# One-sided level scaling, token-layout keys for the state, and a re-sorted plan in a gated linear attention with a low-rank mixer

## The chip, the cores and the metric

The kernel runs on one core of one Trainium2 chip. The metric is the device time of one execution in microseconds; the median of three runs counts. The profile is of one further execution of the same program.

## The reference

Two blocks follow each other, all in float32. The first is a gated linear attention with a complex diagonal gate; B = 4 sequences, H = 8 heads, S = 768 tokens, D = 48 per head.

```python
mag = np.sqrt(a_re * a_re + a_im * a_im)
scale = np.minimum(mag, 0.999) / (mag + 1e-06)
a_re_n, a_im_n = (a_re * scale, a_im * scale)
for t in range(S):
    new_re = ar * S_re - ai * S_im
    new_im = ar * S_im + ai * S_re
    S_re, S_im = (new_re + kv, new_im)          # kv: outer product of k[t] and v[t]
    y[:, :, t] = np.einsum('bhd,bhde->bhe', q[:, :, t], S_re)
```

Its output, with heads side by side, is x with shape (4, 768, 384). The second block mixes tokens by a low-rank product (rank 32) and channels by two layers (384 to 1536 to 384):

```python
h = x.transpose(0, 2, 1) @ U @ V
u = x + h.transpose(0, 2, 1)
out = u + np.maximum(u @ w_ch1, 0.0) @ w_ch2
```

q, k, v and the gates are read with heads outermost. The two weight matrices arrive as 64-bit floats and are converted on the chip (`single`, from `stage` to `w`).

## The kernel before

**Chunks.** Each sequence is cut into chunks of 128 tokens: 24 chunks, 6 to a sequence. Chunks go in groups of two (`GROUPS`); `gates(g)` computes for a group the logarithm of the gate's size (`GL`) and its angle. `within` sums the logarithms from the middle of each block of eight tokens (matrix `mid`, tile `es ps`) and takes the exponentials in both signs (`es`, to scale q and k). `of_blocks` sums them over blocks of many sizes (matrix `total`, 64 columns; tile `tot`), takes the exponential (`E`) and a DMA brings it into the transposed layout as `T`. `angles` sums the angles (`ph`, `F`), and `waves_of` gives sine and cosine (`cs`).

**Prep.** `prep(i)` multiplies q and k by `es` (`weigh`), then by `cs` into `QKC` in token layout (128 tokens by 8 heads by 2 x 64), and TensorE transposes it (`tr`), ScalarE copying into `QK` (112 feature rows by tokens). Queries and keys share one `QKC` buffer.

**Chain.** `chain(i)` computes the causal products of a chunk by levels. After the products within the smallest blocks (`inner`), the queries and keys in `QK` are scaled by `T` so that blocks of double size fit; `times` scales a step of blocks, `grow` a whole level on both sides. There are five such multiplications on VectorE of 112 x 1024 elements for every chunk. The products go through masks into `DG`, by DMA into `AT`, and `corners` adds larger off-diagonal parts. When all scaling is done, the keys in `QK` refer to the end of each half chunk; TensorE transposes them back (`ks ps`), ScalarE copies them to `ks`, and `state` forms `dk` from them and the values `VP`. VectorE carries the running state: `GM` and `G` are the state times `T` plus `dk` (`onward`). `y` comes from `AT` with `VP` and from the queries with `G` and `GM`, and four ScalarE copies write `xo`.

**Mixer.** After each sequence, `mixer(m)` runs for its three pairs of chunks (12 pairs in all): `mixed` (low rank), `uTp`, then `up` and `down`. For the pairs m >= `FEWER` = 6, `up_fewer` replaces `up` by a scheme of 15 block products instead of 18 (tile `few`), with sums on VectorE into the `gate` area and `combine` for the weights. From the second pair on `down_two` does the same for the second layer.

**Order.** No engine's order is written by hand. `Plan` collects every operation with an engine, a cost, reads and writes, and a rank; `order` then runs a list scheduler over these costs and emits one fixed sequence for each engine. Ranks come from the `URGENCY` tables, one number for every stage and chunk. When TensorE has nothing ready before the first mixing, the plan emits a filler product (`spare`). Tiles with a `buffer` count or in a `ring` are handed on only when all their users are done. Semaphores do the waiting on the chip. From group `PAIRED` = 5 on, the levels of two chunks are issued together. Input and `T` transfers go by SyncE's queue, `out` mostly by GpSimd's.

A sequence's first chunk has no state before it, its last one makes none.

Of the kernel before, what the change touches and what calls it, by code (L numbers as in the profile page):

```python
# [26 lines left out]
    "w1": {0: 598.69, 1: 700.38, 2: 561.36, 3: -1085.13, 4: 936.46, 5: 518.46, 6: 1990.31},  # L27
    "w2": {0: 567.2, 2: 731.23, 4: 231.69, 6: 364.31, 8: -127.45, 10: 294.53, 12: 130.99},
    "gates": {0: 523.28, 1: -1082.8, 2: -1138.64, 4: -681.35, 6: 2038.0, 8: 706.57, 10: -2625.84, 12: -1988.48,
        14: 652.13, 16: 729.97, 18: -1261.2, 20: -1293.27, 22: -582.28},  # L30
    "angles": {0: -713.76, 1: 451.99, 2: -1094.23, 4: -1138.42, 6: -877.65, 8: -663.76, 10: 249.87, 12: 258.4,
        14: 730.71, 16: 600.46, 18: 890.52, 20: -1410.11, 22: -1050.09},
    "prep": {0: -1111.25, 1: -1273.83, 2: -1144.23, 3: -1283.97, 4: -1610.93, 5: -400.53, 6: -1090.46, 7: 47.1,
        8: -2361.51, 9: -1335.04, 10: -992.16, 11: -1290.23, 12: 355.91, 13: 718.13, 14: 425.49, 15: -1586.91,
        16: 164.12, 17: -2624.09, 18: -1995.12, 19: 1003.92, 20: 460.11, 21: 683.17, 22: 246.16, 23: 304.03},
    "levels": {0: -1274.23, 1: -77.35, 2: -1122.97, 3: 446.96, 4: -1027.24, 5: 563.68, 6: 533.1, 7: 540.33,
        8: 312.67, 9: -1060.71, 10: -1147.76, 11: 477.09, 12: 434.96, 13: 685.1, 14: 223.22, 15: -902.35,
        16: -1157.33, 17: 559.77, 18: -440.31, 19: 206.74, 20: -992.62, 21: -1506.01, 22: -990.49, 23: -1159.28},
    "rest": {0: 327.21, 1: -703.81, 2: 145.04, 3: 405.93, 4: -948.71, 5: -1277.74, 6: 399.6, 7: 573.79, 8: -1411.6,
        9: -1156.53, 10: -1047.5, 11: 209.25, 12: -915.97, 13: -1258.32, 14: -2795.59, 15: -1131.95, 16: -1080.72,  # L40
        17: -806.17, 18: 376.14, 19: -1093.98, 20: -1201.47, 21: 393.57, 22: -1199.57, 23: 107.96},
# [147 lines left out]
def kernel(  # L189
# [37 lines left out]
    FEWER = B * (S // CH) // 2 - 6  # L227
# [15 lines left out]
    SIZES = (4, 8, 16, 32, 64, 128)  # L243
    NTOT = CH // 2
# [107 lines left out]
    mid = singles.tile([128, CH], FP, name="mid")  # L352
    total = singles.tile([128, NTOT], FP, name="total")
# [32 lines left out]
    GL = [singles.tile([128, GC * DM + 64 - D], FP, name="GL")]  # L386
    nc.gpsimd.memset(GL[0], 0.0)

    tail = singles.tile([128, CH], FP, name="tail")
    nc.gpsimd.tensor_copy(out=tail, in_=ident[:, 127:128].to_broadcast([128, CH]))  # L390
    AT, DG, VP = [], [], []
    QKC = singles.tile([128, H, 2, DP], FP, name="QKC")
    nc.gpsimd.memset(QKC, 0.0)
    GATE = singles.tile([128, 6, GC * DM], FP, name="gate")
    AREA = {nm: GATE[:, n] for n, nm in enumerate(("x", "y", "n", "z", "ar", "ai"))}
# [14 lines left out]
    def constants():  # L410
# [8 lines left out]

        def totals():  # L420

            for n in SIZES:
                m, ends = CH // n, prefix.rearrange("p (b t) -> p b t", t=n)[:, :, n - 1]
                to = total[:, n // 4::n // 2]
                if n == 4:
                    to, frm = (a.rearrange("p (b x) -> p b x", x=4) for a in (to, ends))
                    for x in range(1, 4):
                        nc.gpsimd.tensor_tensor(out=to[:, :, (2, 1, 0, 3)[x]], in0=frm[:, :, x], in1=frm[:, :, x - 1],
                                                op=OP.subtract)
                    nc.gpsimd.tensor_copy(out=to[:, 0:1, 2], in_=frm[:, 0:1, 0])  # L430
                    nc.gpsimd.tensor_tensor(out=to[:, 1:, 2], in0=frm[:, 1:, 0], in1=frm[:, :-1, 3], op=OP.subtract)
                    continue
                nc.gpsimd.tensor_copy(out=to[:, 0:1], in_=ends[:, 0:1])
                if m > 1:
                    nc.gpsimd.tensor_tensor(out=to[:, 1:m], in0=ends[:, 1:m], in1=ends[:, 0:m - 1], op=OP.subtract)
# [28 lines left out]
    def single(p, rank, to, o, pieces):  # L464
# [23 lines left out]
        ACT(c_act(n), rank, lambda: act(o, hi().bitcast(FP), AF.Copy, scale=2.0 ** -112), [raw], [to])  # L488
        ACT(c_act(n), rank, lambda: act(word(x()), lo(), AF.Copy, scale=2.0 ** -29), [raw], [cx])
# [35 lines left out]
    def gates(g):  # L525


        x, y, l, n, z, ar, ai = names = [(nm, g) for nm in ("x", "y", "l", "n", "z", "ar", "ai")]
        first = GROUPS[g][0]

# [14 lines left out]
        def magnitudes_of(lo, hi):  # L545
            t, R1, W = t_of(lo, hi), ("gates", lo), (hi - lo) * DM
            ca, cd = c_act(W), c_dve(W)
            X, Y, L, N = (b + (lo,) for b in (x, y, l, n))
            AR, AI = ([b + (i,) for i in range(lo, hi)] for b in (ar, ai))
            ACT(ca, R1, lambda: act(t(x), t(ar), AF.Square), AR, [X])  # L550
            ACT(ca, R1, lambda: act(t(y), t(ai), AF.Square), AI, [Y])
# [13 lines left out]
            table(ca, R1, lambda: act(t(x), t(x), AF.Ln), [], [X])  # L565
            table(ca, R1, lambda: act(t(x), t(x), AF.Exp, scale=-1.0), [], [X])
            DVE(cd, R1, lambda: mul(t(x), t(x), t(ai)), AI, [X])
            ACT(ca, R1, lambda: act(t(n), t(ar), AF.Sign, bias=tiny), AR, [N])
            for i in range(lo, hi):
                within(i, R1, L)  # L570

# [80 lines left out]
        def waves():  # L652
            buffer(("cs", g), "cs", 2, [128, GC, H, 2, D])
            for part in PARTS[g]:
                waves_of(*part)
# [645 lines left out]
```

## Time and profile before

| | |
|---|---|
| median of three runs | 695.42 us (694.3 to 696.11) |
| the profiled execution | 695.63 us, span 693.8 us |
| TensorE busy | 668.7 us (96%), of it `spare` 53.3 us |
| VectorE busy | 521.5 us (75%), of it the levels' scaling (`QK`) 145.3 us |
| ScalarE busy | 432.1 us (62%), of it the copies to `ks` 23.8 us |
| GpSimd busy | 40.0 us (6%) |
| granted TensorE clock | 1.0 of full speed |

PE is TensorE, DVE VectorE, ACT ScalarE, POOL GpSimd, SP SyncE; PEld is TensorE's weight load, which overlaps its products. A stage line gives the stretch, its length, then busy time (and instruction count) of each engine, the clock, the share of the DMA engines and GB/s. A group line gives line number, engine, operation, tiles (out<-in), shapes and count, then busy time in total and the mean nanoseconds of one, and last the idle time before them with what ended it. Busy time of overlapping instructions is counted once, so busy divided by count can be below the mean of one.

### The profile page before, as it was taken

What the parts mean: (1) busy time and instruction counts of PE and PEld (TensorE: products, weight loads), DVE (VectorE), ACT (ScalarE), POOL (GpSimd) and SP (SyncE); (2) the same over time, 40 slices, a digit from 0 to 9 for tenths busy, and PEclk for the clock granted to TensorE, in tenths of its full rate; (3) what the DMA queues carried; (4) which work ended last, traced back from release to release, by engine and by line L of the source; (5) the groups of instructions that cost most, each with busy time, mean ns of one, the idle gap of its engine ahead of it and who ended that gap; (6) DMA issues with size and microseconds to landing.
All of it is one profiled execution on the core that took longest, in us unless ns stands there. A gap on an engine that the chain in (4) does not pass through costs nothing.

```text
span 693.8 us, 26918 instructions
## 1 busy us (share of the span) xinstructions
PE 668.7 (96%) x12098; PEld 590.5 (85%) x12098; DVE 521.5 (75%) x838; ACT 432.1 (62%) x802; POOL 40.0 (6%) x79
## 2 busy tenths in 40 slices
PE   7899887999999999999999999999999999999998
PEld 7788777786788887978988898889999989899998
DVE  4699998656989978946979588788797876465734
ACT  7999977679968887945968578634425315031230
POOL 5000000000101000010001001000000000000000
PEclk9999999999999999999999999999999999999999
DMA  8746435554514333251433222202111010000000
GB/s 203 187 94 161 90 76 119 131 163 113 114 35 95 80 73 83 47 110 26 78 85 67 49 65 57 60 20 58 26 42 24 14 33 10 23 2 24 7 18 24
DMA packets 163330, 48.32 MB, mean 70 GB/s; under 512 B 153808, under 2 KB 160016, under 8 KB 163216
## 3 DMA queue, kind: packets, MB, share of 16 engines
q1 hardware_dynamic: 161008, 42.26, 27.6%
q0 software_dynamic: 2208, 4.35, 1.8%
q8 instruction: 95, 1.56, 0.9%
q14 instruction: 19, 0.16, 0.1%
HBM read 33.59 MB, written 4.72 MB: 55 GB/s over the span
## 4 chain that ended last, share of the span: by engine, by line
PE 70%; ACT 19%; DVE 6%; issue 3%; DMA 1%; SPq 0%; DVEq 0%; ACTq 0%
PE down L1121 18%; PE few L990 12%; PE up L932 11%; ACT gate L327 7%; PE inner L732 4%; PE tr L698 4%; PE dk L818 3%; PE y L857 2%; ACT QK L701 2%; PE ks ps L803 2%; PE ph L643 2%; PE es ps L576 2%; ACT L324 2%; ACT GL L327 2%; PE y L849 2%
## 5 line engine op out<-in xcount | busy, mean ns | idle before, releaser
L330 DVE TENSOR_TENSOR QK<-QK,T 112x1024 f32<-112x1024 f32 x120 | 145.3, 1217 | 7.7 <-PE inner L732 4.2
L932 PE MATMUL up<-uT,w 128*128 128x256 f32 x432 | 99.2, 381 | 0.2 <-ACT h L327 0.2
L932 PEld LDWEIGHTS up<-uT,w 128*128 128x128 f32 x432 | 80.4, 190 | 12.7 <-ACT h L327 0.6
L1121 PE MATMUL down<-w,h 128*128 128x192 f32 x396 | 72.8, 329 | 1.1 <-issue 1.1
L327 ACT ACTIVATE gate<-gate 128x768 f32<-128x768 f32 (+1 forms) x91 | 70.3, 792 | 2.7 <-DMA gate<-in_a_re_dram 1.6
L701 ACT COPY QK<-tr 112x512 f32<-112x512 f32 x96 | 52.3, 587 | 31.0 <-PE tr L698 30.7
L998 ACT COPY h<-few 128x512 f32<-128x512 f32 x36 | 20.6, 585 | 81.9 <-PE few L990 77.1
L1121 PEld LDWEIGHTS down<-w,h 128*128 128x128 f32 x396 | 63.9, 190 | 3.6 <-issue 2.5
L333 DVE TENSOR_TENSOR h<-few,h 128x512 f32<-128x512 f32 x54 | 37.1, 690 | 34.7 <-PE few L990 33.4
L732 PEld LDWEIGHTS inner<-QK 112*32 112x32 f32 x4608 | 45.7, 109 | 14.1 <-issue 11.3
L732 PE MATMUL inner<-QK 112*32 112x16 f32 (+1 forms) x4608 | 51.2, 190 | 4.3 <-issue 3.0
L698 PE MATMUL tr<-ident,QKC 128*112 128x128 f32 x384 | 52.8, 276 | 2.3 <-DVE QKC L330 1.3
L1245 PE MATMUL spare<-ident 128*128 128x128 f32 x388 | 53.3, 285 | 1.4 <-POOL ident masks.py:199 1.4
L330 DVE TENSOR_TENSOR QKC<-qk,cs 128x768 f32<-128x768 f32 x48 | 45.7, 952 | 11.0 <-PE tr L698 9.0
L1245 PEld LDWEIGHTS spare<-ident 128*128 128x128 f32 x388 | 48.4, 197 | 4.9 <-POOL ident masks.py:199 1.4
L698 PEld LDWEIGHTS tr<-ident,QKC 128*112 128x112 f32 x384 | 41.9, 133 | 9.1 <-ACT QK L701 3.1
L333 DVE TENSOR_TENSOR xo<-down,xo 128x192 f32<-128x192 f32 (+1 forms) x79 | 29.5, 384 | 23.7 <-PE down L1121 23.4
L990 PE MATMUL few<-gate,w 128*128 128x128 f32 x336 | 43.5, 277 | 0.0
L866 ACT COPY xo<-y 64x192 f32<-64x192 f32 x96 | 29.9, 312 | 20.7 <-PE y L857 19.7
L990 PEld LDWEIGHTS few<-gate,w 128*128 128x128 f32 x336 | 40.0, 192 | 0.4
L327 ACT ACTIVATE h<-up 128x512 f32<-128x512 f32 x36 | 21.5, 596 | 29.7 <-PE up L932 29.6
L738 DVE COPY_PREDICATED DG<-mask,inner 128x128 f32<-128x128 int32 (+1 forms) x72 | 24.2, 341 | 17.3 <-PE inner L732 17.0
(130 smaller groups left out, 1241.7 us busy)
## 6 DMA issues: line engine op xcount, KB each, us to landing
stage<-in_moe_w_ch_dram SPq DMA_DIRECT2D x12, 768.0 KB, 5.6
gate<-in_a_re_dram SPq DMA_DIRECT2D x24, 192.0 KB, 3.6
gate<-in_a_im_dram SPq DMA_DIRECT2D x24, 192.0 KB, 3.5
qk<-in_q_dram SPq DMA_DIRECT2D x24, 192.0 KB, 2.7
qk<-in_k_dram SPq DMA_DIRECT2D x24, 192.0 KB, 4.0
VP<-in_v_dram SPq DMA_DIRECT2D x24, 192.0 KB, 3.2
T<-E SPq DMA_DIRECT2D x48, 96.0 KB, 2.5
AT<-DG SPq DMA_DIRECT2D x96, 32.0 KB, 2.1
```

Source lines behind the costliest of these rows:

```text
L327: return nc.scalar.activation(out=o, in_=i, func=f, **kw)
L330: nc.vector.tensor_tensor(out=o, in0=a, in1=b, op=OP.mult)
L333: nc.vector.tensor_tensor(out=o, in0=a, in1=b, op=OP.add)
L698: nc.tensor.transpose(out=get(*ps)[0:DQ, j], in_=get(*qkc)[:, hh * HH + j].rearrange("p u d -> p (u d)")[:, 0:DQ], identity=ident)
L701: ACT(c_act(HH * CH) - 0.05, R1, lambda u=u, hh=hh, ps=ps: nc.scalar.copy(out=get(*QK)[:, u, hh * HH:(hh + 1) * HH], in_=get(*ps)[0:DQ]), ...
L732: nc.tensor.matmul(out=get(*ps)[js, h], lhsT=k_of(h)[:, js], rhs=part(q_of(h)[:, js], "p"), start=True, stop=True, tile_position=(0, j * BLK))
L738: nc.vector.copy_predicated(out=to, mask=part(mask[:, n], "p").unsqueeze(1).to_broadcast(list(to.shape)), data=a if hf < 8 else a.rearrang ...
L866: ACT(c_act(HH * D), RR, lambda r=r, u=u: nc.scalar.copy(out=get(*xi).rearrange("p (a u d) -> p a u d", u=2, d=D)[r * HC:(r + 1) * HC, :, ...
L932: nc.tensor.matmul(out=get(*ps)[:, e], lhsT=w1[:, f, (ff + e) * 128:(ff + e + 1) * 128], rhs=get(*uT)[:, f], start=(f == 0), stop=(f == KD ...
L990: nc.tensor.matmul(out=get(*ps)[:, q], lhsT=w()[:, q * 128:(q + 1) * 128], rhs=v[0](), start=(n == 0 and q == 0), stop=True, skip_group_ch ...
L1121: nc.tensor.matmul(out=get(*to)[:, part], lhsT=x(j), rhs=y[:, j], start=(first and j == 0), stop=(j == KH - 1), skip_group_check=not first)
L1245: nc.tensor.matmul(out=spare[0], lhsT=ident, rhs=ident, start=True, stop=True)
```

## The change

It has these parts:

1. **Levels scale one side.** The `total` matrix has 28 columns instead of 64, for distances from the middle of one block to the middle of another. At each level either the queries or the keys are scaled, not both. A chunk has six multiplications of 512, 512, 512, 256, 512 and 1024 elements (512 for the first chunk of a sequence) instead of five of 1024.
2. **The state's keys are scaled in token layout.** A new matrix `fore` sums the logarithms from the middle of the block of eight to the end of the half chunk (product `ef ps`, one for each chunk, exponential `ef` on ScalarE). `onto_end` multiplies the keys in `QKC` in place, after they were transposed, and `state` takes them from there. The transposes `ks ps`, their copies and the tile `ks` are gone. `QKC` has two buffers, one for queries and one for keys. The state no longer waits for the levels.
3. **The first group's gates on VectorE** (`SPREAD`): the absolute value, the clamp of the logarithm, the sign and the last affine step, two instructions each, go from ScalarE to VectorE. The two conversion copies of the first three weights (`EARLY`) go there too.
4. **The seventh pair** (m = 6) computes `up` with 18 products (`FEWER` = 7).
5. Sine and cosine are made by chunk, with three buffers; `z` shares the area of `y`, and the area that `z` had holds part of `ef`; `tail` is a broadcast view of `ident`; `GL` has no padding; some costs of the plan differ by 0.05 to 0.1.
6. **All `URGENCY` numbers differ**, so the order on each engine differs throughout.

```diff
-    FEWER = B * (S // CH) // 2 - 6
+    FEWER = B * (S // CH) // 2 - 5
...
-    SIZES = (4, 8, 16, 32, 64, 128)
-    NTOT = CH // 2
+    EARLY, SPREAD = 3, (0,)
+
+    TA, TC, TQ, TK, TF, TH, NTOT = 0, 8, 12, 16, 18, 26, 28
...
-    QKC = singles.tile([128, H, 2, DP], FP, name="QKC")
-    nc.gpsimd.memset(QKC, 0.0)
+    QKC = []
+    for n in range(2):
+        QKC.append(singles.tile([128, H, 2, DP], FP, name="QKC%d" % n))
+        nc.gpsimd.memset(QKC[n], 0.0)
...
+        def ahead():
+
+            for r in range(0, CH, HC):
+                n = HC // 8
+                nc.gpsimd.tensor_tensor(
+                    out=fore[:, r:r + HC].rearrange("p (b t) -> p b t", t=8), in0=prefix[:, r + HC - 1:r + HC].unsqueeze(1).to_broadcast([128, n, 8]),
+                    in1=e[:, r // 8:r // 8 + n, 3:4].to_broadcast([128, n, 8]), op=OP.subtract)
+        POOL(0.7, ("load", 2), ahead, reads=[("prefix", 0)], writes=[("fore", 0)])
...
+            if p < EARLY:
+                DVE(one, rank, lambda o_=o_, i_=i_, scale=scale: nc.vector.tensor_scalar(
+                    out=o_(), in0=i_(), scalar1=scale, scalar2=None, op0=OP.mult), [raw], [at])
+            else:
+                ACT(c_act(n) + 0.1, rank, lambda o_=o_, i_=i_, scale=scale: act(o_(), i_(), AF.Copy, scale=scale), [raw], [at])
...
+            if on_dve:
+                DVE(c_one(W), R1, lambda: nc.vector.tensor_scalar(out=t(n).bitcast(U32), in0=t(ar).bitcast(U32), scalar1=0x7FFFFFFF, scalar2=None,
+                                                                  op0=OP.bitwise_and), AR, [N])
+            else:
+                ACT(ca, R1, lambda: act(t(n), t(ar), AF.Abs), AR, [N])
...
+            pf, ef = ("ef ps", i), ("ef", i)
+            psum(pf, "T", [128, DM], [128, 512])
+            summed(fore, ("fore", 0), pf, ef)
+            table(c_act(DM), R1, lambda: act(get(*ef), get(*pf), AF.Exp, scale=-1.0), [pf], [ef])
...
+        def onto_end():
+            a = get("qkc", 2 * i + 1)[:, :, :, 0:D]
+            mul(a, a, heads(get("ef", i)).unsqueeze(2).to_broadcast([128, H, 2, D]))
+        DVE(c_dve(2 * DM), ("rest", i), onto_end, [("ef", i)], [("qkc", 2 * i + 1)])
...
-        times(RL, 4, 16, 8, H * CH - 8, 0)
+        times(RL, 0, 8, TA, (16, 8, 1), (1, 8, 0))
         yield from inner(1, 8)
-        times(RL, 4, 16, 0, H * CH + 8, 2)
-        grow(RL, 8)
+        times(RL, 1, 0, TA, (16, 8, 1), (1, 8, 0))
+        times(RL, 0, 16, TC, (32, 4, 1), (1, 16, 0))
         yield from inner(0, 16)
...
-        grow(RR, 16)
+        times(RR, 1, 0, TK, (HC, 2, 1), (1, 16, 0))
+        times(RR, 0, 32, TQ, (HC, 2, 2), (16, 2, 1), (1, 16, 0))
...
-        grow(RR, 32)
+        lo = 0 if c else HC
+        times(RR, 0, lo, TF + lo // 16, (16, (CH - lo) // 16, 1), (1, 16, 0))
...
-        ks, dk = ("ks", i), [("dk", (i, r)) for r in range(2)]
-        buffer(ks, "ks", 1, [128, H, DQ])
+        ks, dk = ("qkc", 2 * i + 1), [("dk", (i, r)) for r in range(2)]
         buffer(mid_G, "GM", 1, [DQ, H, D])
-        rows_k = HC if last else CH
-        for hh in range(2):
-            ps = ("ks ps", (i, hh))
-            psum(ps, "A", [128, HH, DQ], [128, HH, CH])
-
-            def turn(hh=hh, ps=ps):
-                for j in range(HH):
-                    nc.tensor.transpose(out=get(*ps)[0:rows_k, j], in_=k_of(hh * HH + j)[:, 0:rows_k], identity=ident[0:DQ, 0:DQ])
-            PE(0.4, RR, turn, [QK], [ps], takes=[ks], steps=HH)
-            ACT(0.54, RR, lambda hh=hh, ps=ps: nc.scalar.copy(out=get(*ks)[0:rows_k, hh * HH:(hh + 1) * HH], in_=get(*ps)[0:rows_k]),
-                [ps], [ks + (hh,)])
...
-                        nc.tensor.matmul(out=get(*dk[r])[x:end, h], lhsT=get(*ks)[at, h, x:end], rhs=get(*VPi)[at, h],
+                        nc.tensor.matmul(out=get(*dk[r])[x:end, h], lhsT=get(*ks)[at, h, x // DP, 0:end - x], rhs=get(*VPi)[at, h],
```

In the listing of the changed program, all `ef` products for chunks 0 to 7 stand before the first `up`, and all 168 `spare` too; VectorE's instruction for the keys of a chunk stands behind `onto_end` of the chunk before.

## The prediction

> **What bounds the kernel now.** I read the page's busy shares and slices first, then the busy time by stage, the same stages for the `spare` products alone, the chain that ended last, and last the groups by form, for the price of single instructions. The page:
>
> ```profile
> PE 668.7 (96%) x12098; PEld 590.5 (85%) x12098; DVE 521.5 (75%) x838; ACT 432.1 (62%) x802; POOL 40.0 (6%) x79
> PE   7899887999999999999999999999999999999998
> DVE  4699998656989978946979588788797876465734
> ACT  7999977679968887945968578634425315031230
> PE 70%; ACT 19%; DVE 6%; issue 3%; DMA 1%; SPq 0%; DVEq 0%; ACTq 0%
> ```
>
> TensorE looks like the bound everywhere, but part of its 668.7 us is filler. Busy time by stage (all engines, then `spare` alone; PE is the first busy column, then PEld, DVE, ACT):
>
> ```profile
> 0.00:40.00 40.00, 34.02 (x449) 30.67 (x450) 24.05 (x42) 34.35 (x62) 10.06 (x32) 1.00 0.77 187
> 40.00:100.00 60.00, 54.80 (x1426) 46.35 (x1424) 57.39 (x77) 55.53 (x100) 0.00 (x0) 1.00 0.44 100
> 100.00:140.20 40.20, 34.06 (x933) 28.46 (x932) 30.79 (x45) 29.27 (x59) 0.00 (x0) 1.00 0.56 137
> 140.20:300.00 159.80, 157.28 (x2821) 129.71 (x2821) 131.14 (x186) 130.70 (x229) 10.02 (x14) 1.00 0.40 89
> 300.00:589.00 289.00, 287.05 (x5734) 257.74 (x5730) 223.74 (x369) 159.27 (x315) 15.11 (x24) 1.00 0.22 47
> ...
> 0.00:40.00 40.00, 23.95 (x183) 23.11 (x184) 1.00 0.77 187
> 40.00:100.00 60.00, 19.48 (x144) 17.20 (x142) 1.00 0.44 100
> 100.00:140.20 40.20, 9.85 (x64) 8.06 (x64) 1.00 0.56 137
> ```
>
> So there are two kernels. Until 140.2 us, where the first `up` starts, 53.3 us of TensorE's 122.9 are filler: this ramp (chunks 0 to 5) is set by ScalarE (first 40 us: 34.4 busy) and VectorE (40 to 100 us: 57.4 of 60). After it TensorE is busy 157.3 of 159.8 and 287.1 of 289.0 us: there its own work is the time, and VectorE's and ScalarE's savings are mostly hidden.
>
> Prices from the chain in order of time (start, us, what) and from the groups:
>
> ```profile
> 5.96 1.60 DVE gate L553
> 161.98 1.29 PE es ps L576 x4
> 187.13 2.59 PE up L932 x12
> 634.35 13.55 PE few L990 x120
> ...
> L330 DVE TENSOR_TENSOR QK<-QK,T 112x1024 f32<-112x1024 f32 x120 | 145.3, 1217 | 7.7 <-PE inner L732 4.2
> L803 PE MATMUL ks ps<-ident,QK 112*128 112x112 f32 (+1 forms) x192 | 23.8, 261 | 0.0
> L1245 PE MATMUL spare<-ident 128*128 128x128 f32 x388 | 53.3, 285 | 1.4 <-POOL ident masks.py:199 1.4
> ```
>
> An fp32 product leaves two records and a transpose one: two `es ps` products take 1.29 us, six `up` 2.59, sixty `few` 13.55, one transpose 23.8/192 = 0.124, one `spare` 53.3/194 = 0.275.
>
> **Part by part.** *TensorE after the ramp.* 18 chunks lose eight `ks ps` transposes each: 144 x 0.124 = -17.9 us. 16 of the 24 new `ef ps` products come after the first `up`: 16 x 0.645 = +10.3. The seventh pair returns from 60 products (13.55) to 36 (6 x 2.59 = 15.5): +2.0. `tot` goes from 64 to 28 columns; if its 1.08 us per chunk pair of 32 records followed columns it would give 5.5 us over 18 chunks, but `y` with 48 columns costs the same 1.07 for 32 records, so I take 0 and keep -5.5 for the range. `dk`, `tr`, `y`, `inner` keep their counts. Sum -5.6.
>
> *VectorE.* 1024 elements take 1.217 us, 512 take 0.687 (the `few` adds), 768 take 0.952; 256 comes to 0.42. A chunk's levels go from 5 x 1.217 = 6.08 to 4 x 0.687 + 0.42 + 1.217 = 4.38 (3.85 for a sequence's first), 43 us in all. `onto_end` gives back 24 x 0.952 = 22.8. The seventh pair saves 9 adds and its sums, 9.1. The weights' six copies cost 3.3 at 0.555 (the contiguous 768-wide row; 5.7 if the stepped input runs at 0.952), the first group 2.8. Net -23; in the ramp alone -10.8 + 5.7 + 3.3 + 2.8 + 0.5 (one `F` more) = +1.5. But the additions for weights and first group fall into the first 40 us, where VectorE has 16 us free (two thirds of it; the third weight comes later), while the levels fall into 40 to 140: about -4.6 in the stage where VectorE is full.
>
> *ScalarE, ramp.* `ks` copies -6.4, weights -6 x 0.93, first group eight instructions of 0.51 to 0.61 = -4.6, narrower `E` -0.9; `ef` +8 x 0.45, `cs` by chunk instead of by group +2.5 (two 384-wide 0.529 for one 768-wide 0.842), one gate and one `F` pulled ahead +1.4. Sum -10.0, most of it in the first 80 us, where ScalarE is 90% busy.
>
> *The ramp.* The two limits give -4.6 and -10. The listing of the changed program has 168 `spare` instead of 194, all before the first `up`, and the rest of TensorE's work there is the same within 1 us (48 transposes out, 8 `ef` in): 26 x 0.275 = -7.2. I take -7; ends -14 (both limits add, since they lie in different stretches) and +3 (VectorE's +1.5 and one waiting `dk` per pair).
>
> *The first group on VectorE.* The chain shows what speaks against it: the clamp at 5.96 us took 1.59 where the same shape later took 0.35, while GpSimd worked through its constants until 10.7 us. Five or so of the eight moved instructions fall into that stretch; off the chain they cost nothing, on it 1.24 each. I take one hit before and one after, 0, with +2.5 (two more) for the range. The Trainium skill, "SBUF — State Buffer", section "SBUF: two separate sides", says that VectorE in a two-port mode and GpSimd lock each other out for a whole instruction; with GpSimd's instructions of some 0.3 us an estimate by that rule would be +1.5 for five hits; the 1.59 agrees with such a lock, the second clamp's 0.35 at 9.6 us, with GpSimd still at work, does not show one.
>
> *Stalls after the ramp.* Visible idle of TensorE from 140 to 589 us is 2.5 + 2.0 us, plus stretched pace at VectorE-full places. VectorE sheds some 24 us there: I take -3; ends -8 (the idle gone and as much again of pace) and +9 (new waits below). `T<-E` transfers shrink from 96 to 42 KB with 2.5 us to landing: 0, they run far ahead; at worst a share of 2.5 us once. All order tables are new, so every queue is re-sorted; no row prices this, and the +9 contains it.
>
> *New waits.* `QKC` has two buffers, and the keys' one is now held until `dk` of that chunk: the next chunk's keys wait on VectorE behind `onto_end`, TensorE's `dk` and what is queued before it, and everything behind on VectorE waits too. From one pair to the next the listing has 12 to 36 us of VectorE work between; inside a pair it has 0.95, 4.3, 3.6, 3.4, 10.2, 2.1, 1.9, 0.4, 2.4, 1.1, 1.7 and 12.4 us. `dk` alone is 1.07. So some pairs wait 1 to 2 us; after the ramp TensorE has other products to cover that.
>
> Sum: the profiled execution took 695.6 us (span 693.8 and 1.8 around it; the median of the runs is 695.4). 695.6 - 5.6 - 7 - 3 = 680.0.
>
> **Rivals.**
> (a) *The ramp stays.* For it: VectorE's ramp work is +1.5, and VectorE is full from 40 to 100. Against: 26 fewer fillers and ScalarE's -10. Then -5.6 alone: 690.
> (b) *More goes.* Both ramp limits add (-14) and stalls fall by 8: 695.6 - 27.6 = 668; with `tot` by columns 662.5. For it: the chunk's state no longer waits for its levels, so the chain from chunk to chunk is shorter.
> (c) *Slower: the keys' buffer becomes the loop.* `dk` also needs the running state's buffer `GM`, which `y` of the chunk before frees, and that waits for `AT` to land: 2.1 (AT) + 1.07 (y) + 0.6 (two copies) + 1.07 (dk) + 0.95 (keys) + 1.02 (eight transposes) + 0.59 (copy) = 7.4 us once per pair, less the cover listed above. In the three ramp pairs 6.5 + 3.1 + 3.8 = 13.4, all on the path; in the nine others 39 us on VectorE, of which TensorE's other products hide perhaps three quarters, leaving 10: 680 + 23 = 703. It decides from (697.5 - 680)/12 = 1.5 us per pair that reach TensorE. Against it: covers of 3.4 us or more in five pairs.
> (d) *It does not do what it says.* `ef` at its group's mean (19.2/24 = 0.8) costs 12.8, TensorE saves only 3.1, and the ramp grows by VectorE's 1.5: 694, no change.
>
> **How the numbers follow.** Forecast (680, about 673 to 686) 0.52; (a) 0.19; (b) 0.16; (c) 0.10; (d) 0.03. A difference under 0.3% (2.1 us) can't be told from none. Faster: 0.52 + 0.19 + 0.16 = 0.87; same 0.03; slower 0.10. The range goes from 664 (nearly all of (b)) to 695 (over (a) and (d)) and leaves out (c).
>
> **What would show it.** Right: the first `up` near 133 us; `spare` near 46 us; no `ks ps`, `ef ps` near 15 to 19 us; the levels near 102 us in 144 instructions; TensorE over 98% busy from there, its `few` near 68. Wrong: `up` starting after 140; VectorE's keys product waiting for `dk` by over 1.5 us a pair; TensorE idle over 15 us after the ramp; moved `tensor_scalar` rows of over 1 us before 11 us on the chain.

## The result, and the profile after

The changed kernel takes 688.9 us (median of twenty runs, 685.63 to 694.58) where the kernel before takes 695.69 in the runs beside it: a ratio of 0.9915, interval 0.9894 to 0.9936. That is -6.8 us where -15.6 was forecast: the direction is right, the size less than half. The profiled execution took 688.27 us (span 686.5).

The page of the changed kernel (busy time, slices, shares of the chain that ended last):

```profile
PE 664.0 (97%) x11854; PEld 576.5 (84%) x11854; DVE 495.9 (72%) x882; ACT 413.8 (60%) x791; POOL 40.9 (6%) x81
PE   8999998999999999999999999999999989999998
PE 78%; DVE 8%; ACT 6%; issue 2%; DVEq 0%; ACTq 0%
```

VectorE has lost 25.6 us (forecast 23) and ScalarE 18.3, and ScalarE's share of the chain has fallen from 19% to 6%. But TensorE is busy only 4.7 us less. The stages, cut at the first `up`, which now starts at 131.4 us:

```profile
0.00:40.00 40.00, 35.38 (x440) 31.21 (x441) 29.29 (x57) 28.20 (x52) 10.93 (x34) 1.00 0.75 182
40.00:100.00 60.00, 55.12 (x1525) 44.26 (x1523) 56.91 (x93) 57.14 (x111) 0.00 (x0) 1.00 0.51 111
...
131.40:686.50 555.10, 544.37 (x9135) 478.14 (x9134) 384.95 (x693) 303.25 (x581) 29.00 (x46) 1.00 0.22 48
```

The last line's counterpart before:

```profile
140.20:693.80 553.60, 545.81 (x9297) 484.99 (x9295) 409.27 (x676) 312.90 (x583) 29.98 (x47) 1.00 0.24 53
```

In the first 40 us ScalarE's busy time fell from 34.4 to 28.2 and VectorE's rose from 24.1 to 29.3, as forecast. Counted from the first `up` itself (140.06 us before, 131.42 now) the ramp is 8.6 us shorter. All the rest is 1.3 us **longer**, although it has 162 records less on TensorE (a record is one matmul line of the profile) and 24 us less on VectorE. That stretch holds the miss. The groups that answer to the ones shown of before:

```profile
L331 DVE TENSOR_TENSOR QK<-QK,T 112x512 f32<-112x512 f32 (+1 forms) x144 | 99.8, 715 | 7.4 <-PE corners L830 4.7
L1288 PE MATMUL spare<-ident 128*128 128x128 f32 x336 | 48.2, 291 | 1.9 <-POOL ident masks.py:199 1.4
L611 PE MATMUL ef ps<-GL,fore 128*128 128x384 f32 x48 | 19.9, 497 | 1.4 <-POOL fore L427 1.4
L331 DVE TENSOR_TENSOR QKC<-qk,cs 128x768 f32<-128x768 f32 x48 | 45.0, 953 | 9.2 <-issue 3.4 <-ACT cs L328 3.0 <-PE dk L855 2.5
```

The third line is new (its wait is for GpSimd's `fore`, once, in the ramp). The end of the last line is the wait of slower rival (c): 2.5 us in the whole run. For TensorE I summed by tile the time from one instruction's start to the next one's, after the first `up`, which is what an instruction costs in a queue that never rests:

| after the first `up`, us | before | after | difference | forecast |
|---|---|---|---|---|
| `ks ps` | 14.97 | 0 | -15.0 | -17.9 |
| `ef ps` | 0 | 10.78 | +10.8 | +10.3 |
| `up` and `few` | 180.19 | 183.42 | +3.2 | +2.0 |
| `tot` | 9.0 | 8.2 | -0.8 | 0 |
| `dk` and `down` | 196.56 | 199.95 | +3.4 | (stalls, -3) |

The other tiles come to -0.3 together. Where about half of the third line comes from is seen in TensorE's timeline around 560 us (start, busy, what, and in brackets the idle time before it with what ended it):

```profile
558.10 1.22 PE L784 MATMUL inner<-QK 112*32 112x16 f32 x122
561.39 0.25 PE L784 MATMUL inner<-QK 112*32 112x16 f32 x6 [2.08 <-issue]
561.57 1.16 PE L1027 MATMUL few<-gate,w 128*128 128x128 f32 x8
562.57 1.77 PE L1027 MATMUL few<-uT,gate 128*128 128x128 f32 x8
564.13 1.91 PE L1027 MATMUL few<-gate,w 128*128 128x128 f32 x8
```

In the midst of the 128 records of one `inner` TensorE stands for 2.08 us, and nothing that the profile shows releases it ("issue"). One microsecond later eight products of `few` take 1.77 and 1.91 us where eight took 1.16. The stages there (clock is the third number from the end):

```profile
562.00:564.00 2.00, 2.00 (x15) 2.00 (x14) 1.86 (x5) 0.59 (x1) 0.00 (x0) 0.68 0.03 8
564.00:566.00 2.00, 2.00 (x11) 2.00 (x11) 0.89 (x2) 0.00 (x0) 0.00 (x0) 0.50 0.02 4
```

The granted clock falls to 0.50; the trace's clock records have it so for 3.41 us from 562.72 on. What is lost is about 1.6 us on top of the 2.08: the 32 products of `few` take 5.40 us to the start of the next tile, and 3.77 in the version with wide fillers below. The profiled execution of before has no such fall at all.

**Which record pauses.** The count in a stage line that starts at zero is the number of matmul records so far. Cut at the beginning of two pauses (0.98 and 2.08 us), for the changed kernel:

```profile
0.00:71.00 71.00, 63.26 (x1238) 53.31 (x1238) 58.31 (x105) 57.13 (x107) 10.93 (x34) 1.00 0.64 154
0.00:561.36 561.36, 542.31 (x10766) 459.37 (x10766) 427.50 (x738) 381.60 (x728) 36.00 (x72) 1.00 0.35 78
```

and for the kernel before, at its pauses of 1.17 and 1.29 us in the ramp:

```profile
0.00:80.10 80.10, 70.10 (x1363) 61.08 (x1364) 62.15 (x92) 72.48 (x129) 10.06 (x32) 1.00 0.63 151
0.00:119.10 119.10, 102.98 (x2379) 89.79 (x2379) 98.32 (x142) 105.77 (x192) 10.06 (x32) 1.00 0.56 132
```

1238 = 9 x 127 + 95, 10766 = 84 x 127 + 98; 1363 = 10 x 127 + 93, 2379 = 18 x 127 + 93. The longer pauses of both programs stand at the same places of the *queue*, whatever work stands there, and nearly all where the 127 records before were short: `inner`, `dk` and `y` use 0.01 to 0.03 us each (122 of `inner` in 1.22 us, 32 of `dk` in 1.07). Counted over the traces of all the runs here, 120 of the 283 block ends behind 127 records of under 4 us show a pause of over 0.3 us, and 8 of the 1012 behind 127 records of over 5 us. The work behind the end can be long: `down` waits 0.75 us at record 9620 of the changed kernel and 1.08 us at record 10761 of the one before. The page's DMA queue for instructions (packets, MB, share), before and after:

```profile
q8 instruction: 95, 1.56, 0.9%
```

```profile
q8 instruction: 93, 1.52, 0.9%
```

12098 records are 95.3 x 127, and 11854 are 93.3 x 127. So I read it as TensorE waiting for the next block of its own instructions when it has run through one faster than the next arrives. The traces bear this out. All 145 pauses by issue of over 0.3 us behind the first 200 records, in all runs here, stand between record 88 and 99 of a block of 127. (Among the first 200 there is at most one, before `ph`, of 0.71 us or less.) Each of them ends 1.17 to 1.66 us after a packet of this queue (16,384 bytes) has landed; at the 1409 block ends without a pause that distance spreads from 0 to 26 us.

### The profile page after: what moved, and what is told of

The parts are those of the page before. It is cut to its first block, busy times and chain, and to the rows that moved or that the text cites. A ratio compares the mean times of both kernels' runs of the same rounds, so it can differ in the third digit from the quotient of the medians.

```text
span 686.5 us, 26452 instructions
## 1 busy us (share of the span) xinstructions
PE 664.0 (97%) x11854; PEld 576.5 (84%) x11854; DVE 495.9 (72%) x882; ACT 413.8 (60%) x791; POOL 40.9 (6%) x81
## 4 chain that ended last, share of the span: by engine, by line
PE 78%; DVE 8%; ACT 6%; issue 2%; DVEq 0%; ACTq 0%
PE down L1158 18%; PE up L969 15%; PE few L1027 10%; PE inner L784 6%; PE tr L745 4%; PE dk L855 3%; PE y L894 3%; PE es ps L611 2%; PE down L1115 2%; PE ph L689 2%; PE ef ps L611 2%; PE spare L1288 2%; ACT gate L328 2%; PE y L886 2%; PE tot L647 1%
## 5 line engine op out<-in xcount | busy, mean ns | idle before, releaser
L969 PE MATMUL up<-uT,w 128*128 128x256 f32 x504 | 116.1, 382 | 0.0
L969 PEld LDWEIGHTS up<-uT,w 128*128 128x128 f32 x504 | 94.0, 190 | 15.2 <-DVE uT L959 0.3
L331 DVE TENSOR_TENSOR QK<-QK,T 112x512 f32<-112x512 f32 (+1 forms) x144 | 99.8, 715 | 7.4 <-PE corners L830 4.7
L1035 ACT COPY h<-few 128x512 f32<-128x512 f32 x30 | 17.4, 584 | 70.6 <-PE few L1027 62.5
L784 PEld LDWEIGHTS inner<-QK 112*32 112x32 f32 x4608 | 45.1, 109 | 17.3 <-issue 13.1
L334 DVE TENSOR_TENSOR h<-few,h 128x512 f32<-128x512 f32 x45 | 31.1, 692 | 34.3 <-PE few L1027 30.4
L745 PEld LDWEIGHTS tr<-ident,QKC 128*112 128x112 f32 x384 | 42.2, 134 | 10.5 <-ACT QK L748 3.3
L1288 PE MATMUL spare<-ident 128*128 128x128 f32 x336 | 48.2, 291 | 1.9 <-POOL ident masks.py:199 1.4
L1288 PEld LDWEIGHTS spare<-ident 128*128 128x128 f32 x336 | 43.5, 201 | 5.7 <-issue 1.5
L328 ACT ACTIVATE h<-up 128x512 f32<-128x512 f32 x42 | 24.9, 592 | 33.2 <-PE up L969 33.0
L1158 PE MATMUL down<-stage 128*128 128x192 f32 x198 | 36.8, 327 | 0.7 <-issue 0.7
L1027 PE MATMUL few<-gate,w 128*128 128x128 f32 x280 | 37.2, 282 | 0.0
L790 DVE COPY_PREDICATED DG<-mask,inner 128x128 f32<-128x128 int32 (+1 forms) x72 | 24.5, 343 | 14.6 <-PE inner L784 14.5
```

The lines of the kernel that those rows point to most:

```text
L328: return nc.scalar.activation(out=o, in_=i, func=f, **kw)
L331: nc.vector.tensor_tensor(out=o, in0=a, in1=b, op=OP.mult)
L334: nc.vector.tensor_tensor(out=o, in0=a, in1=b, op=OP.add)
L745: nc.tensor.transpose(out=get(*ps)[0:DQ, j], in_=get(*qkc)[:, hh * HH + j].rearrange("p u d -> p (u d)")[:, 0:DQ], identity=ident)
L784: nc.tensor.matmul(out=get(*ps)[js, h], lhsT=k_of(h)[:, js], rhs=part(q_of(h)[:, js], "p"), start=True, stop=True, tile_position=(0, j * BLK))
L969: nc.tensor.matmul(out=get(*ps)[:, e], lhsT=w1[:, f, (ff + e) * 128:(ff + e + 1) * 128], rhs=get(*uT)[:, f], start=(f == 0), stop=(f == KD ...
```

## The experiments

My theory after the result: the ramp went as forecast, and after it the relief of VectorE was worth nothing, while a pause of TensorE and the half clock after it took away 4 to 5 us. Rivals: the `QKC` buffer's wait costs more than its 2.5 us show (c); the new order itself is worse after the ramp; the 18 products cost more than forecast. All prices are against the changed kernel's 688.9 us (first `up` 131.4, rest 555.1) unless told otherwise; ratios are against the kernel before on the same chip. That kernel took 694.4 to 694.8 us beside the experiments and 695.7 beside the changed kernel, so some 1 us of a difference in microseconds can be the chip's.

**Undoing parts and tables.** The keys' wait, with two more `QKC` buffers (cleared by VectorE) and each engine's order as it was:

```diff
-    for n in range(2):
+    for n in range(4):
         QKC.append(...)
...
-            ring(qkc, "qkc", QKC)
+            plan.buffer(qkc, "qkc", 2)
+            makers[qkc] = lambda n=plan.turn[qkc] % 4: QKC[n]
```

> The changed kernel with four QKC buffers, keys and queries alternating between two each, with every engine's order unchanged: takes away the wait of the next chunk's keys for dk. Theory that this wait is where the missing 8 us of the stage after the ramp went: 3 to 8 us less, 681 to 686. Instruction-block theory and prices only: within 1 us of the changed kernel, since TensorE has other products to run; at most 1 us less in the ramp.

Measured 687.32 us (684.41 to 692.26), ratio 0.9908 [0.9879, 0.9937]; first `up` 131.8, a pause of 1.80 at 560.48 us again with the clock at 0.50 behind it. By the medians the buffer's wait is worth 1.6 us, by the ratios nothing clear of the noise: rival (c), which asked for 23, is out.

The seventh pair back to 15 products (planned anew):

```diff
-    FEWER = B * (S // CH) // 2 - 5
+    FEWER = B * (S // CH) // 2 - 6
```

> The changed kernel with the seventh pair by 15 products again (the order is planned anew with the same tables). Prices only: TensorE saves 3.2 us by the trace (2.0 by the prediction's rows), VectorE pays 9 us of sums, hidden: 685.5 to 687. If the seventh pair was moved because VectorE's sums did not hide: 690 or more. New order: up to 3 us either way on top.

711.89 us, ratio 1.0259 [1.0236, 1.0281], far from what the products cost: first `up` 131.1, rest 578.1. TensorE runs dry between 460 and 507 us; the first part of it:

```profile
460.00:480.00 20.00, 13.27 (x359) 10.34 (x357) 12.84 (x23) 15.36 (x35) 1.36 (x2) 0.83 0.22 48
```

and its waits there are for VectorE (tile and line waiting, who releases it: us in all, times, longest):

```profile
PE inner L784 <- DVE QK L331: 7.5, 4, 5.4
PE tr L745 <- DVE QKC L331: 6.0, 6, 1.6
```

By the listing, the sums for `few` of that pair live in the areas of the gates and of `ef`, which are handed on in order; so the pair's `few` comes only behind the last group's gates. In the trace the last `up` starts at 432.7 us and the first `few` at 507.3, and in between TensorE runs out of mixing to cover the chain. This tells of a plan, not of the 18 products. Their price alone I took in the old program, where the plan stays close:

```diff
-    FEWER = B * (S // CH) // 2 - 6
+    FEWER = B * (S // CH) // 2 - 5
```

> The kernel before with the seventh pair by 18 products, planned anew with its own tables. By TensorE's prices +2.0 us: 697 to 698. If the seventh pair's sums hold VectorE or the gates' area up: 690 to 694. Order of the new plan: up to 3 us either way on top.

697.87 us, ratio 1.0039 [1.0019, 1.0058]: +3.1 (2.7 by the ratio), as expected. The term of +2.0 has the right sign and size, somewhat too small here.

Both tables of ranks, exchanged: the changed kernel with the old numbers, and the old kernel with the new ones.

```diff
-URGENCY = {"w1": {0: 68.6, 1: 298.27, ...
+URGENCY = {"w1": {0: 598.69, 1: 700.38, ...
```

> The changed kernel planned with the URGENCY tables of the kernel before. If the tables matter little (the prediction's 9 us upper end for all re-sorting): within 9 us of 688.9. If each set of tables fits only the program for which it stands: 700 to 730, with TensorE idle on VectorE or DMA after the ramp.

> The kernel before planned with the changed kernel's tables. Tables matter little: 690 to 705. Tables fit only their program: 705 to 740. If the new tables alone bring the gain: 685 to 690.

720.72 us, ratio 1.0385 [1.0363, 1.0406], and 722.26, ratio 1.0401 [1.0382, 1.042]. The first `up` starts at 145.6 and 159.5 us. A table fits the program that it was made with, and another program loses 28 to 32 us by it. Undoing one part under the given tables mixes the part's price with that loss, so the further runs leave the order alone where they can.

**The two limits of the ramp.** First the levels' old cost on VectorE: an operation of 1.69 us on a tile of its own ahead of each chunk's first scaling, the order unchanged.

```diff
+    ballast = singles.tile([128, 1480], FP, name="ballast")
+    nc.vector.memset(ballast, 1.0)
...
+                if t == TA and u == 0:
+                    mul(ballast[0:112], ballast[0:112], ballast[0:112])
```

> The changed kernel with one extra multiplication of 112 x 1480 elements on a spare tile (1.69 us by the rows' slope) beside the first scaling of every chunk: VectorE gets back the time that one-sided scaling saved, every engine's order unchanged. Prediction's theory (VectorE's savings count in the ramp where it is full, are mostly hidden after it): the first up 4.6 to 10 us later than 131.4, the stage after the ramp 0 to 3 us longer: 694 to 701. Rival: VectorE's relief does nothing even in the ramp (ScalarE sets it): 689 to 691. Rival: VectorE sets the stage after the ramp too: 18 chunks times 1.7 = 30 us there, over 715.

717.31 us, ratio 1.0317 [1.0267, 1.0366]:

```profile
140.50:711.20 570.70, 546.81 (x9135) 477.77 (x9133) 411.93 (x711) 303.71 (x581) 28.94 (x46) 1.00 0.22 47
```

The ramp is 9.1 us longer for six operations of 1.69 (10.1): VectorE's time there is on the path, as forecast. The clock falls three times in that ramp, so not all of the 9.1 need be VectorE's own time. But the rest is 15.6 us longer for 18 x 1.69 = 30.4, where next to nothing was expected. Then the first group back on ScalarE:

```diff
-    EARLY, SPREAD = 3, (0,)
+    EARLY, SPREAD = 0, ()
```

> The changed kernel with the first group's gates and the first weights' copies on ScalarE again (planned anew with the same tables). Prediction's theory (ScalarE sets the first 40 us; 10.2 us of its 10.0 net come from these moves): the first up 3 to 8 us later, time 692 to 698. Rival (VectorE alone sets the ramp): the first up 3 to 6 us earlier, since VectorE loses 6 us of work: 684 to 687.

706.45 us, ratio 1.0155 [1.0111, 1.0199]. The first `up` starts at 139.2, +7.8, within what was expected; ScalarE has 119.5 us busy up to there, 9 us more. The other +10.8, which takes the time beyond the 698 expected, lies after the ramp, where this change touches no instruction. The orders were planned anew: TensorE waits 1.5 us for `AT` at 293.7 us, and the clock is 0.50 from 296.9 to 310.6, which alone can cost 6.8 us.

**The position of the instruction blocks.** If the pauses sit at counts of 127 in the queue, more or fewer fillers in the ramp move them through the work behind. Sixteen records more, as short products at the very start:

```diff
+    idle()
+    for _ in range(7):
+        nc.tensor.matmul(out=spare[0][:, 0:16], lhsT=ident, rhs=ident[:, 0:16], start=True, stop=True)
     for n in plan.order():
```

> The changed kernel with one more filler and seven filler products of 16 columns ahead of TensorE's queue: 16 more records, every engine's order else the same, so that TensorE's blocks of 127 records end at other places. Instruction-block theory (the 2.08 us pause at 561.4 us and the half clock behind it are a block that came late behind short products): by the pace of the trace this shift leaves no block end inside the products of the last chunks' levels; no pause over 1 us after 540 us, granted clock 1.000 in nearly all runs, time 685.5 to 687. Rival, prices only (transposes 0.104 not 0.124, seventh pair 3.2 not 2.0): the time stays at 688.9, clock between 0.99 and 1.0 from run to run as before. Rival, heat or chance sets the clock: the same.

692.63 us (690.14 to 696.68), ratio 0.9985 [0.9966, 1.0003]: worse, not better. The fillers were not free (first `up` 134.25), and the shift put the boundaries into other `inner` blocks:

```profile
0.00:505.15 505.15, 486.77 (x9620) 406.78 (x9621) 381.52 (x643) 362.49 (x686) 32.61 (x66) 1.00 0.38 84
0.00:567.10 567.10, 546.35 (x10766) 463.22 (x10766) 427.35 (x738) 381.71 (x728) 35.94 (x72) 1.00 0.35 77
```

```profile
501.76 1.22 PE L784 MATMUL inner<-QK 112*32 112x16 f32 x122
505.19 0.25 PE L784 MATMUL inner<-QK 112*32 112x16 f32 x6 [2.22 <-issue]
```

Record 10766 pauses again, now at 567.2 us and 16 records earlier in the work (22 of the 128 records of that `inner` come behind it, not 6); 9620 = 75 x 127 + 95 is a new one, after which the clock falls to 0.69 and 0.50 (506 to 510 us). Neither this pause of 1.49 us nor a third, 1.89 us at 272.1, had a fall behind it. The number of the record decides, not the work: the time and the place of the pauses (none over 1 us after 540 us) were forecast wrongly, the mechanism stood. A shift by 52 records in the same way (25 short products):

> The same with 52 more records, the shift for which the pace of the trace gives the most late blocks after the ramp. Instruction-block theory: more pauses by issue after 131 us (3 to 6 us instead of 3.3 us), granted clock lower, time 689.5 to 693. Prices only, or chance: 688.9, as without the shift.

699.11 us, ratio 1.008 [1.0059, 1.0101]. The 26 products in front moved the first `ph` from 21.5 to 30.1 us and the first `up` to 141.9, which is +10.5 by itself; the rest is 557.1 with pauses of 1.43, 0.82 and 1.69 us and the clock down from 248.1 to 251.5 and from 568.9 to 572.3. Fillers added at the start cost more than they could bring. Taking them away is the other direction: of the first forty fillers every second is left out (40 records fewer).

```diff
+    fillers = 0
     for n in plan.order():
-        (plan.ops[n][4] if n >= 0 else idle)()
+        fillers += n < 0
+        if n >= 0 or fillers > 40 or fillers % 2:
+            (plan.ops[n][4] if n >= 0 else idle)()
```

> The changed kernel without every second of its first 40 fillers: 40 records fewer ahead of everything, every order else unchanged. By the trace's pace, summed over block ends (4.0 us minus the time of the 127 records before, where that is positive), the stage after the ramp has 7.2 instead of 14.8, close to the least of all shifts. Instruction-block theory: pauses by issue after the ramp fall below 2 us in all, clock 1.000 in most runs, time 684 to 686.5. Prices only, or chance: 688.9 and clocks between 0.99 and 1.0. If the missing fillers let the clock fall in the first 20 us: up to 2 us later from there.

684.79 us (683.87 to 686.62), ratio 0.9855 [0.9823, 0.9886]. In the ramp the clock falls (0.50 from 10.7 to 17.5 and from 89.2 to 92.6 us) and the first `up` starts 2.9 us later, but the rest takes 550.5, 4.6 less, at a clock of 1.00. To keep TensorE busy in the ramp and still have 40 records fewer, twenty wide fillers instead of forty:

```diff
+        if n >= 0 or fillers > 40:
+            (plan.ops[n][4] if n >= 0 else idle)()
+        elif fillers % 2:
+            nc.tensor.matmul(out=both, lhsT=ident, rhs=ident.unsqueeze(1).to_broadcast([128, 2, 128]), start=True, stop=True)
```

> The changed kernel with its first 40 fillers of 128 columns as 20 of 256: 40 records fewer, as in the run without every second filler, but without idle time in between. Instruction-block theory: the stage after the ramp as in that run (550.5 us, pauses under 2 us), the clock full in the first 20 us, the first up back at 131.5 to 133: 681.5 to 684. Prices only, or chance: 688.9. If the late first up of that run came from the blocks in the ramp and not from the missing fillers: 134, time 684 to 685.

**683.76 us** (682.47 to 688.05), ratio 0.987 [0.9843, 0.9897]: the fastest version with the whole computation. It is 5.1 us under the changed kernel by the medians and 5.4 by the profiled executions. Against the kernel before on its own chip it gains 10.7 us where the changed kernel gained 6.8, which leaves 3.9 (3.1 by the ratios): 3 to 5 us in all. Its ramp is as long as the changed kernel's, and the rest takes 549.7. The long stretch where mixing and chunks overlap, with wide fillers and in the changed kernel:

```profile
131.40:574.00 442.60, 438.71 (x8369) 376.29 (x8369) 325.93 (x566) 280.12 (x542) 24.11 (x37) 1.00 0.27 57
```

```profile
131.40:580.00 448.60, 441.26 (x8373) 378.70 (x8372) 327.24 (x566) 280.71 (x543) 24.12 (x37) 1.00 0.26 56
```

The same work in 442.6 instead of 448.6 us, without one fall of the clock and with no pause in `inner` over 0.43 us, and nothing but the fillers differs in the program. With four `QKC` buffers on top:

> The same with four QKC buffers, orders unchanged. The keys' wait for dk costs nothing once TensorE has no pauses: the same as the run before it within 1 us. If the wait costs: 1 to 3 us less.

687.21 us, ratio 0.9904 [0.9881, 0.9926]: not better, and beyond the 1 us expected. At the two records of the ramp where the run before pauses 1.19 and 0.91 us (1618 and 1998) it now pauses 1.44 and 2.22, the clock falls behind both, and the first `up` starts at 137.0. The rest takes 549.9 as without the buffers, so after the ramp they bring nothing. The same for the kernel before, with thirty wide fillers for its first sixty:

```diff
+        if n >= 0 or fillers > 60:
```

> The kernel before with its first 60 fillers of 128 columns as 30 of 256: 60 records fewer, orders unchanged. By its trace's pace the sum over late block ends goes from 4.8 to 10.3 in the ramp and from 11.8 to 18.4 after it (its own position is close to its best). Instruction-block theory: more pauses by issue, some half-clock stretches, 698 to 706. If position matters to the changed kernel alone: 694 to 696.

701.11 us, ratio 1.0087 [1.0062, 1.0113], first `up` 141.9, the clock down at 50.4 to 53.8, 84.5 to 87.9 and 111.8 to 115.2 us, the rest 2.6 us longer. So the kernel before stood better than at this other position and the changed one worse than with 40 records fewer: part of what was compared is where 127-record blocks happened to end.

**What VectorE's time is worth after the ramp.** Relief, on the version with wide fillers: `onto_end` scales 2 of the 48 features only.

```diff
-            mul(a, a, heads(get("ef", i)).unsqueeze(2).to_broadcast([128, H, 2, D]))
+            mul(a[:, :, :, 0:2], a[:, :, :, 0:2], heads(get("ef", i))[:, :, 0:2].unsqueeze(2).to_broadcast([128, H, 2, 2]))
```

> The changed kernel with the wide fillers, and the keys' scaling in token layout cut to 2 of 48 features (the other 46 are left unscaled, so the state is another one): VectorE has some 0.7 us less for each chunk, every order unchanged. If VectorE still holds TensorE after the ramp: 3 to 10 us less than 683.8. If its relief is hidden there: 0 to 3 us less, of it most in the ramp.

682.61 us (682.22 to 685.68), ratio 0.9835 [0.981, 0.9861].

```profile
131.80:680.50 548.70, 541.91 (x9135) 475.95 (x9133) 370.68 (x693) 302.85 (x581) 28.91 (x46) 1.00 0.22 49
```

VectorE has 12.9 us less than the version with wide fillers has after its ramp (383.6), and the stretch is 1.0 us shorter. And burden, the 1.69 us of the earlier experiment on the same version:

> The changed kernel with the wide fillers and the extra multiplication of 1.69 us for each chunk. If the 15.6 us after the ramp of the earlier run were VectorE's: again 12 to 16 us longer than 549.7 there, 703 to 709 in all. If they were pauses and half clock: 0 to 6 us longer there, 692 to 698 in all.

709.86 us, ratio 1.0214 [1.019, 1.0239]: the ramp +6.3, the rest 570.5, +20.8 for 30.4, more than expected. So 12.9 us of relief bring 1 and 30.4 us of burden cost 16 to 21. TensorE's waits for VectorE after the first `up` grow from 1.5 to 14.6 us in all, and 10.2 us at half clock can cost up to 5.1 more. The two longest sums name whom the burden reaches:

```profile
PE es ps L613 <- DVE GL L596: 3.8, 3, 1.6
PE inner L786 <- DVE QK L331: 3.8, 5, 1.5
```

## Why the prediction was right and wrong

**The ramp: right, the number partly by luck.** -8.6 us for -7. The first `up` was forecast near 133 and came at 131.4, `spare` near 46 and took 48.2. Both limits that the text named are limits: the two runs with the ballast lose 9.1 and 6.3 us there for 10.1 of VectorE's time, and the first group on ScalarE costs 7.8. But the -7 was counted as fillers that fall away, and they gave 5.1 us instead of 7.2. TensorE's whole busy time in the ramp fell by 3.0 us; the other 5.6 are idle time (17.3 to 11.7), which no line had priced. Of the price for the moved gate steps, one hit was forecast and one is seen, VectorE's first such instruction:

```profile
3.63 1.44 DVE L578 TENSOR_SCALAR gate<-gate 128x384 uint32<-128x384 uint32 x1 [2.62 <-DMA gate<-in_a_re_dram]
5.62 0.39 DVE L578 TENSOR_SCALAR gate<-gate 128x384 uint32<-128x384 uint32 x1
```

The second, two microseconds later with GpSimd still at work (its constants now end at 12.2 us), took 0.39. The weights' copies with stepped input took 0.553 us each, the contiguous price that I chose and not the 0.952 of the other end. One wait was missed: `ef ps` for `fore` on GpSimd, 1.4 us, once.

**TensorE's own work after the ramp: the signs right, one term mis-sized.** The `ks ps` transposes were priced at 23.8/192 = 0.124 us, busy time by count; from start to start they take 14.97/144 = 0.104. One product lasts 0.261 us in that row, so the busy time of a group reaches into the next tile's products. So -15.0 instead of -17.9: 2.9 us of the miss. `ef ps` came to 0.67 for 0.645 (+0.5), and `tot` to -0.8 for 0: the narrower product hardly changed its pace, as `y` with its 48 columns had suggested. The seventh pair was about right: 2.2 us with wide fillers, 3.1 in the old program, and in the changed kernel 1.6 when what half clock cost (1.6) is left out.

**The stalls after the ramp: the step that failed.** I took -3, because VectorE sheds 24 us there. Without the terms above (-15.0 + 10.8 + 1.6 - 0.8 = -3.4), the measured +1.3 leaves +4.7 for this step. The profiled execution is 8.3 us over the forecast: the stalls +7.7, the prices +2.2, the ramp -1.6. Two reasons. First, the text credited TensorE's visible idle time of 4.5 us to VectorE, and it was hardly VectorE's. The waits of TensorE in the kernel before, after its first `up` (line waiting, who ended it: us in all, times, longest):

```profile
PE inner L732 <- issue: 1.4, 3, 0.7
PE down L1121 <- issue: 1.1, 1, 1.1
PE ph L643 <- ACT QK L701: 0.8, 2, 0.6
PE uTp L920 <- DVE xo L333: 0.3, 2, 0.2
```

VectorE ended 0.3 us of them; 2.5 are pauses at block ends. So the relief is worth almost nothing (1.0 us for 12.9). The opposite is not so: added VectorE time makes the stretch longer by half to two thirds of it. The slack on one engine can't be read in both directions from one row; that a fixed order has cover for its planned costs and no more would explain it, but was not tested by itself.

Second, something that no line of the text priced: the change takes 244 records out of the queue, all blocks of 127 end elsewhere, and one boundary fell into an `inner` late in the run. After the ramp the changed kernel has 3.3 us of pauses by issue for 2.5 before, 1.6 us lost at half clock for none, and 4.1 us of waits for ScalarE and VectorE for 1.9: these make up the +4.7 but for 0.1. With the wide fillers the pauses are 0.6 us, no half clock is left, and the waits are 3.3. There `down` takes 2.1 us less than in the changed kernel, `inner` 1.7, `few` 1.0 and `dk` 0.7. What then remains to the forecast is 2.8 us in the profiled execution (682.8 for 680.0): the prices +2.8, the stalls +1.6 (they came to -1.4), the ramp -1.6.

**The clock.** In the traces of all runs 19 pauses by issue lasted 1.40 us or more. 11 of them were followed within 1.8 us by a clock of 0.50, and 8 were not, the longest of all (2.51 us, in the first run with the ballast) among these. The traces' clock records show what decides. Every stretch at 0.50 within a run lasts 3.41 us or a multiple of it, and so does every stretch at full clock between two of them, so the clock changes only on a grid of 3.41 us. The 2.08 us pause of the changed kernel lies whole in one window of that grid (559.31 to 562.72), and the clock falls at the window's end. A boundary of the grid cuts the 1.89 us pause (at 271.22) and the 2.51 us one (at 586.47). Of the 22 windows at full clock with over 1.6 us of TensorE's idle time, whoever ended it, 21 were followed by half clock; of the 3351 with less, 8.

The Trainium skill, "TensorE: Matmul & The Clock Gate", "Part 1: The HAM clock gate", says that the clock goes to half after an idle window of about 3.4 us, and that the window runs freely, so that its phase differs from run to run. The length and the fixed grid agree with these records. A window idle throughout is not needed here, since no pause by issue was longer than 2.51 us; the measurement decides. The free phase would fit what the runs show: the changed kernel's mean clock was 0.989 to 1.000 from run to run, and its time follows, 685.6 to 688.3 us in the seven runs at 1.000 and 693.9 to 694.6 at 0.989 to 0.990. That the scatter comes from such pauses in runs without a profile was not shown.

**The rivals.** (c), the slower one, is out: `dk` ended 2.5 us of waits of the keys' product in the whole run, and two more buffers change the time by 1.6 us by the medians. (a), the ramp that stays, and (d), no change, are out by the first `up`, though the 690 of (a) lies nearer to the measured time than the forecast does. Of the 7 us more in the ramp that (b) asked for, 1.6 came, and the stalls went the other way. Of the wrong signs that the text listed three did not come: the first `up` at 131.4, no 1.5 us of waiting for `dk` in a pair, TensorE idle for 10.7 us from the first `up` to the end. The fourth is open: one moved row took 1.44 us at 3.63 us, but the chain that ended last begins at 35.7 us. The signs could not catch what happened, because a slower clock counts as busy.

**Open.** Why 120 of the 283 blocks behind short records came late and the others in time; how much of the added waits for ScalarE and VectorE belongs to the pauses and how much to the order; and what each part would be worth in an order planned for it alone, since the given tables fit the whole only.

## What to carry to other kernels

Count a queue's instructions as well as their microseconds: with thousands of short products, a change of a few dozen records anywhere moves the block boundaries through all work behind, here worth 3 to 5 us (0.4 to 0.8%), about half of what the change itself gained, or more. So before a small gain or loss is put down to an edit, shift the queue by some harmless records and measure again. Before idle time is credited to an engine, list who ended it. Price a pipelined instruction by the distance between starts, not by busy time over count. And in a packed static order, take relief off the bounding engine at zero and added time at its full price until a run shows otherwise.

## What the hardware did that was not expected

- TensorE can stand for up to 2.5 us once every 127 matmul records, counted from the program's start (102 of the 145 pauses at record 93 to 95 of a block), mostly where the records before were short, and goes on 1.17 to 1.66 us after a packet of its instruction queue has landed. The same record numbers pause in different programs (1238 and 10766, within one or two).
- After such a pause the granted clock may be 0.50 for 3.41 us, with TensorE busy all the time: eight products of 1.16 us took up to 1.91. It follows nearly always where over 1.6 us of idle time lie in one window of the 3.41 us grid (21 of 22), and seldom else (8 of 3351).
- A product of 28 columns goes at nearly the pace of one of 64 (0.8 us less of 9.0 for the same number of records).
